# V weights loaded in two halves, the first V sum split around the next transposes and copied by ScalarE, one epsilon moved to VectorE

## Chip, cores, metric

One core of one Trainium2 chip. The metric is the device time of one launch in microseconds (us); lower is better. A profiled execution gives the span, from the first to the last instruction, which is 1.7 us less than the time.

## The reference, cut to what matters

```python
xn = layernorm(x)                       # x: 2048 x 512, bf16
qkv = xn @ wqkv                         # 512 x 1536; 32 heads of 16
p = softmax(where(window of 256 keys, q k^T / 4, -1e9))
out = x + (p v) @ wo + ((xn @ w_gate) * (xn @ w_up)) @ w_down      # F = 1792
```

The kernel works in chunks of 512 rows, each of four blocks of 128. The change is to the opening: the first chunk's normalisation, its transposes and its V projection.

## The kernel before

TensorE is called PE, ScalarE ACT, VectorE DVE, GpSimd POOL, SyncE SP. The parts that matter:

```python
# setup(): loads in order, all issued by SyncE
for lo, hi in ((0, 1), (1, 2), (2, 4)):
    nc.sync.dma_start(out=self.x[:, lo:hi, :], in_=xv[:, lo:hi, :])
for lo in (1024, 512, 0):                         # V, K, Q columns of Wqkv, 512 KB each
    nc.sync.dma_start(out=self.Wqkv[:, :, lo:lo + 512], in_=wq[:, :, lo:lo + 512])
# ... Wg, Wu, x 4:8, Wd, Wo ...
for lo, hi in ((8, 10), (10, 12), (12, NT)):
    nc.sync.dma_start(out=self.x[:, lo:hi, :], in_=xv[:, lo:hi, :])
# ...
self.keep_busy(40)                                # dummy 128x128 matmuls on zeros

def norm_transpose(self, t, by_dma):              # PE transposes, ScalarE copies to xnT
    # ...
    n = 2 if b == 0 else 4                        # block 0 in two pieces
    for lo in range(0, 4, n):
        ps = self.ps_m.tile([128, n, 128], BF16, tag="M", name="xTp")
        for k in range(n):
            nc.tensor.transpose(ps[:, k, :], xn[:, 128 * (lo + k):128 * (lo + k) + 128], self.ident[:])
        nc.scalar.activation(out=self.xnT[T][:, b, lo:lo + n, :], in_=ps[:], func=ACT.Copy)

def proj_v(self, t, ks=range(4), engine=None):    # V of block t: four matmuls over k, one copy
    # ...
    for k in ks:
        nc.tensor.matmul(ps[:], lhsT=self.xnT[T][:, b, k, :],
                         rhs=self.Wqkv[:, k, 1024:1536], start=(k == 0), stop=(k == 3))
    # ...

def first_chunk(self):
    # ... statistics, epsilon and power, xn of blocks 0 to 2 ...
    self.norm_transpose(0, False)
    self.keep_busy(8)
    for b in range(4):
        if b < 3:
            self.norm_transpose(b + 1, False)
        self.proj_v(b, engine="act" if b == 2 else "dve")
        if b == 0:
            self.norm_apply(3)
    self.proj_qk(0, 0, 1, engine="dve")           # K
    self.proj_qk(0, 0, 0, engine="act")           # Q
    self.swap_halves(0, self.nc.scalar)           # two transfers issued by ScalarE
    self.proj_qk(0, 1, 1, engine="dve")
```

After that the instructions of all engines follow a fixed list, the same in both kernels but for one x load.

The softmax here doesn't subtract the row's maximum and nothing guards it: scores larger than these inputs give would overflow.

## Time and profile before

| | kernel before |
|---|---|
| three timed runs, us | 264.74, 264.87, 264.91 |
| the profiled run: time, span | 265.39, 263.7 |
| V weights issued, landed in that run | 2.17, 7.13 |
| first V matmul, first K matmul in that run | 7.26, 11.35 |

How to read it: the prediction shows the lines. The first matmul of the K projection, which I call K below, is the end of the stretch that the change touches. From there PE works through the same list in both kernels.

### The profile page before, as it was taken

How to read it: one execution, taken by the hardware profiler on the slowest of the kernel's cores; microseconds unless marked ns; L12 is line 12 of the kernel's file. 1: busy time of each engine (PE TensorE's matmuls, PEld its weight loads, DVE VectorE, ACT ScalarE, POOL GpSimd, SP SyncE). 2: the span in 40 equal slices, each digit the busy share in tenths (PEclk: the TensorE clock that was granted, in tenths of full speed). 3: DMA queues.
4: the chain of work that ended last, by engine and by line, in shares of the span. 5: the costliest groups of instructions: out<-in, count | busy, mean ns of one | idle time of the engine just before them, and what ended most of it. 6: DMA issues, size and time to landing. Idle time of an engine off the chain costs nothing.

```text
span 263.7 us, 8896 instructions
## 1 busy us (share of the span) xinstructions
PE 259.4 (98%) x3890; PEld 120.9 (46%) x3890; DVE 175.1 (66%) x342; ACT 175.5 (67%) x141; POOL 116.9 (44%) x278
## 2 busy tenths in 40 slices
PE   8999999999999999999999999999999999999996
PEld 8444444444444544444544454444544445444453
DVE  6677888877845497567873669766685135977344
ACT  3376788888856866677776566767777546787600
POOL 6216342425457645334456644544453451463600
PEclk9999999999999999999999999999999999999999
DMA  6999921220002600002001310000100100000002
GB/s 180 378 357 340 281 29 22 24 47 4 0 25 57 84 2 0 4 0 47 5 0 42 81 45 2 0 2 19 32 4 0 42 21 22 5 0 2 4 2 80
DMA packets 19431, 15.12 MB, mean 57 GB/s; under 512 B 7360, under 2 KB 19392, under 8 KB 19392
## 3 DMA queue, kind: packets, MB, share of 16 engines
q1 hardware_dynamic: 18848, 14.26, 19.9%
q8 instruction: 30, 0.49, 0.8%
q10 hardware_dynamic: 544, 0.30, 0.4%
q14 instruction: 9, 0.07, 0.1%
HBM read 9.70 MB, written 2.10 MB: 45 GB/s over the span
## 4 chain that ended last, share of the span: by engine, by line
PE 96%; DMA 2%; SPq 0%; issue 0%; DVE 0%
PE gp L395 19%; PE up L406 19%; PE psd L428 17%; PE qkp L251 11%; PE S L312 10%; PE acc L366 6%; PE vp L239 5%; PE psd L434 5%; PE L L428 2%; DMA Wqkv<-in_A_wqkv_dram 2%; PE L L434 1%; PE L L366 0%; SPq L74 0%; PE xTp L209 0%; DVE x L444 0%
## 5 line engine op out<-in xcount | busy, mean ns | idle before, releaser
L319 ACT ACTIVATE P<-S 128x2048 bf16<-128x2048 f32 x75 | 140.7, 1876 | 50.6 <-PE S L312 46.8
L158 POOL TENSOR_SCALAR_AFFINE_SELECT P<-P 64x256 bf16<-64x256 bf16 x224 | 100.9, 450 | 126.3 <-ACT P L319 112.1
L395 PE MATMUL gp<-xnT,Wg 128*128 128x512 bf16 x224 | 60.1, 380 | 0.0
L406 PE MATMUL up<-xnT,Wu 128*128 128x512 bf16 x224 | 59.1, 380 | 0.0
L411 DVE TENSOR_TENSOR hT<-up,gsb 128x512 bf16<-128x512 f32 x56 | 38.3, 685 | 19.3 <-PE up L406 13.7
L428 PE MATMUL psd<-Wd,hT 128*128 128x512 bf16 (+1 forms) x210 | 48.0, 369 | 0.0
L343 DVE TENSOR_TENSOR P<-P,diag 128x512 bf16<-128x512 bf16 (+1 forms) x75 | 29.4, 392 | 6.1 <-ACT P L319 6.1
L428 PEld LDWEIGHTS <-hT 128*128 128x128 bf16 x238 | 21.3, 98 | 25.1 <-issue 2.9
L406 PEld LDWEIGHTS <-Wu 128*128 128x128 bf16 x224 | 20.5, 98 | 25.4 <-issue 2.5
L395 PEld LDWEIGHTS <-Wg 128*128 128x128 bf16 x224 | 20.3, 98 | 25.1 <-issue 1.9
L312 PE MATMUL S<-Q,K 16*64 16x320 bf16 (+4 forms) x720 | 31.0, 260 | 0.0
L312 PE MATMUL S<-Q,Ko 32*64 32x320 bf16 (+4 forms) x720 | 30.9, 260 | 0.0
L251 PE MATMUL qkp<-xnT,Wqkv 128*128 128x512 bf16 x128 | 29.9, 380 | 0.0
L230 ACT ACTIVATE gsb<-gp 128x512 bf16<-128x512 f32 x39 | 22.9, 596 | 8.2 <-PE gp L395 7.4
L312 PEld LDWEIGHTS <-K 16*64 16x64 bf16 x720 | 12.1, 103 | 30.7 <-issue 30.7
L372 DVE STREAM_TRANSPOSE at<-acc 128x512 f32<-128x512 f32 x30 | 19.1, 688 | 8.9 <-PE acc L366 8.9
L444 DVE TENSOR_TENSOR x<-psd,x 128x512 bf16<-128x512 f32 (+1 forms) x15 | 9.7, 655 | 15.7 <-PE psd L434 15.7
L251 PEld LDWEIGHTS <-Wqkv 128*128 128x128 bf16 x128 | 11.7, 98 | 14.5 <-issue 1.6
L366 PE MATMUL acc<-P,VS 64*32 64x320 bf16 (+4 forms) x672 | 17.7, 253 | 0.0
L366 PE MATMUL acc<-P,V 64*32 64x320 bf16 (+4 forms) x672 | 17.5, 253 | 0.0
L366 PEld LDWEIGHTS <-V 64*32 64x32 bf16 x720 | 15.1, 91 | 2.2 <-issue 1.6
L239 PE MATMUL vp<-Wqkv,xnT 128*128 128x512 bf16 x64 | 15.3, 380 | 0.5 <-DMA Wqkv<-in_A_wqkv_dram 0.5
(54 smaller groups left out, 200.2 us busy)
## 6 DMA issues: line engine op xcount, KB each, us to landing
out_dram<-x SPq DMA_DIRECT2D x15, 128.0 KB, 1.7
Wg<-in_B_w_gate_dram SPq DMA_DIRECT2D x2, 896.0 KB, 11.4
Wu<-in_B_w_up_dram SPq DMA_DIRECT2D x2, 896.0 KB, 13.7
Wd<-in_B_w_down_dram SPq DMA_DIRECT2D x1, 1792.0 KB, 17.2
Wqkv<-in_A_wqkv_dram SPq DMA_DIRECT2D x3, 512.0 KB, 5.9
x<-in_A_x_dram SPq DMA_DIRECT2D x2, 512.0 KB, 8.7
VS<-V SPq DMA_DIRECT2D x6, 144.0 KB, 2.6
x<-in_A_x_dram SPq DMA_DIRECT2D x3, 256.0 KB, 6.6
```

What stands on the lines that cost most here:

```text
L158: nc.gpsimd.affine_select(out=v, in_=v, pattern=pattern + [[1 if diag else -1, 64]], compare_op=ALU.is_ge if diag else ALU.is_gt, fill=0.0 ...
L230: nc.scalar.activation(out=out, in_=in_, func=ACT.Copy)
L239: nc.tensor.matmul(ps[:], lhsT=self.xnT[T][:, b, k, :], rhs=self.Wqkv[:, k, 1024:1536], start=(k == 0), stop=(k == 3))
L251: nc.tensor.matmul(ps[:], lhsT=self.Wqkv[:, k, lo:lo + 128], rhs=self.xnT[T][:, :, k, :], start=(k == 0), stop=(k == 3))
L312: nc.tensor.matmul(S[64 * par:64 * par + 64, e, col:col + n], lhsT=(self.Ko if par else self.K)[U, c][rows, keys], rhs=self.Q[T, c][rows, ...
L319: nc.scalar.activation(out=P[:, :, 0:col], in_=S[:, :, 0:col], func=ACT.Exp, scale=0.25)
L343: self.nc.vector.tensor_tensor(out=v, in0=v, op=ALU.min, in1=self.diag.unsqueeze(1).unsqueeze(1).to_broadcast([128, 4, n, 64]))
L366: nc.tensor.matmul(accs[par][32 * e:32 * e + 32, q:q + n], lhsT=v, rhs=P[rows, e, col:col + n], start=(i == 0), stop=(i == len(todo) - 1), ...
L395: nc.tensor.matmul(ps[:], lhsT=self.Wg[:, k, 128 * f:128 * f + 128], rhs=self.xnT[T][:, :, k, :], start=(k == 0), stop=(k == 3))
L406: nc.tensor.matmul(ps[:], lhsT=self.Wu[:, k, 128 * f:128 * f + 128], rhs=self.xnT[T][:, :, k, :], start=(k == 0), stop=(k == 3))
L411: nc.vector.tensor_tensor(out=self.hT[T, f][:], in0=ps[:], in1=self.gsb[:], op=ALU.mult)
L428: nc.tensor.matmul(ps, lhsT=self.hT[T, f][:, 128 * b:128 * b + 128], rhs=self.Wd[:, f, c0:c1], start=(f == 0), stop=False)
```

## The change

The intent: start the first V sum on two quarters of the weights before the rest has landed; put the next transposes between its halves; free VectorE of one copy, so that xn of block 3 comes sooner; shorten the chain to that xn by adding its epsilon on VectorE.

```diff
-        for lo in (1024, 512, 0):
-            nc.sync.dma_start(out=self.Wqkv[:, :, lo:lo + 512], in_=wq[:, :, lo:lo + 512])
+        for lo, ks in ((1024, slice(0, 2)), (1024, slice(2, 4)), (512, slice(0, 4)), (0, slice(0, 4))):
+            nc.sync.dma_start(out=self.Wqkv[:, ks, lo:lo + 512], in_=wq[:, ks, lo:lo + 512])
@@
-        for lo, hi in ((8, 10), (10, 12), (12, NT)):
+        for lo, hi in ((8, 12), (12, NT)):
@@ norm_scale: ve = var + epsilon
-        (nc.gpsimd if t else nc.vector).tensor_scalar(...)
+        (nc.vector if t in (0, 3) else nc.gpsimd).tensor_scalar(...)
@@ first_chunk
-        for b in range(4):
-            if b < 3:
-                self.norm_transpose(b + 1, False)
-            self.proj_v(b, engine="act" if b == 2 else "dve")
-            if b == 0:
-                self.norm_apply(3)
+        self.proj_v(0, (0, 1))
+        first = self.cur
+        self.norm_transpose(1, False)
+        self.cur = first
+        self.proj_v(0, (2, 3), engine="act")
+        self.norm_apply(3)
+        self.proj_v(1, (0, 1))
+        self.norm_transpose(2, False)
+        self.proj_v(1, (2, 3), engine="dve")
+        self.norm_transpose(3, False)
+        self.proj_v(2, engine="act")
+        self.proj_v(3, engine="dve")
```

More of the change, by code (lines that the diff above doesn't have):

```diff
@@ L178, in norm_scale @@
         ve = self.small.tile([128, n], F32, tag="ve", name="ve")
-        (nc.gpsimd if t else nc.vector).tensor_scalar(out=ve[:], in0=mv[:, :, 1], scalar1=1e-5, scalar2=None,
+        (nc.vector if t in (0, 3) else nc.gpsimd).tensor_scalar(out=ve[:], in0=mv[:, :, 1], scalar1=1e-5, scalar2=None,
                                                       op0=ALU.add)
```

## The prediction

> **What bounds the kernel now.** I read the busy table first, then the chain that ended last, then the waits of TensorE, then the first 15 us in order of time. From the page:
>
> ```profile
> span 263.7 us, 8896 instructions
> PE 259.4 (98%) x3890; PEld 120.9 (46%) x3890; DVE 175.1 (66%) x342; ACT 175.5 (67%) x141; POOL 116.9 (44%) x278
> PE   8999999999999999999999999999999999999996
> ```
>
> TensorE (PE) is busy 259.4 of 263.7 us, and only the first and last slice of forty (6.6 us each) show less than 9. No other engine passes 67%. The waits of PE, whole run:
>
> ```profile
> PE wps L127 <- DVE idle L94: 1.1, 1, 1.1
> PE vp L239 <- DMA Wqkv<-in_A_wqkv_dram: 0.5, 1, 0.5
> ```
>
> So PE waits twice: 1.1 us before its first dummy matmul, and 0.5 us before the first V matmul, for the V columns of Wqkv. From then to the last few us it is fed without a break. The chain in order of time, first 20 us, says the same:
>
> ```profile
> 2.17 4.96 DMA Wqkv<-in_A_wqkv_dram
> 7.12 0.14 issue
> 7.26 1.02 PE vp L239 x4
> 8.28 0.22 PE xTp L209 x4
> ```
>
> The V weights are issued at 2.17, land at 7.13, and PE starts on them 0.13 later. After that the chain is PE to the tail. Hence an earlier start of the projections is worth its full length at the end, but nothing else in this change touches the path. What the opening looks like, from the timeline (engine, line, operation; PE, ACT and DVE lines that matter):
>
> ```profile
> 5.74 0.76 PE L127 MATMUL wps<-idle 128*128 128x128 bf16 x8
> 5.88 0.41 DVE L190 TENSOR_SCALAR xn<-x,mv,rs 128x512 bf16<-128x512 bf16 x1
> 6.35 0.40 PE L209 MATMUL xTp<-ident,xn 128*128 128x128 bf16 x4
> 6.78 0.60 ACT L210 ACTIVATE xnT<-xTp 128x512 bf16<-128x512 bf16 x1 [0.36 <-PE xTp L209]
> 7.26 1.02 PE L239 MATMUL vp<-Wqkv,xnT 128*128 128x512 bf16 x4 [0.51 <-DMA Wqkv<-in_A_wqkv_dram]
> 8.93 0.40 DVE L190 TENSOR_SCALAR xn<-x,mv,rs 128x512 bf16<-128x512 bf16 x1
> 9.39 0.40 PE L209 MATMUL xTp<-ident,xn 128*128 128x128 bf16 x4
> 9.62 1.89 PE L239 MATMUL vp<-Wqkv,xnT 128*128 128x512 bf16 x8
> 11.35 2.75 PE L251 MATMUL qkp<-xnT,Wqkv 128*128 128x512 bf16 x12
> ```
>
> The start times give PE's true pace: the eight V matmuls from 9.62 to the first qkp at 11.35 take 1.73/8 = 0.216 us each, and four transposes (8.12 to 8.34, 9.39 to 9.62) 0.22 us together. The printed lengths add about 0.17 of pipeline at the end of each group. Between 7.26 and 11.35 lie 4.09 us; its work is 16 x 0.216 + 2 x 0.22 = 3.90 us. So two idle pieces exist before the K projection: 0.69 us between the transposes of block 1 (6.35 + 0.22 = 6.57) and 7.26, and some 0.19 us before the transposes of block 3 at 9.39. That last one waits for xn of block 3, which VectorE makes only at 8.93, behind the V copy of block 0. From 11.35 on the order of instructions is the same in both kernels on every engine (I compared the two built programs), apart from one x load.
>
> **What the Trainium skill says.** "TensorE: Matmul & The Clock Gate", section "Wait — 56ns, not 53.3ns?", gives 215.7 ns start to start for 512 columns and 55.6 for 128 when warm; the trace has 0.216 and 0.22/4 = 0.055, so it agrees. "DMA: Bandwidth & Descriptors", section "Why a DMA increments its semaphore by 16 and not by 1", says that only the full count means that all data landed. So today's first V matmul needs all 512 KB though it reads a quarter; two transfers give two completions. The trace agrees as far as it goes: one release at 7.13. The same page, "Anatomy of one DMA", puts most of the fixed cost in the receipt after the last byte, so half the bytes is not half the 4.96 us. "ScalarE: Activation LUTs", section "What ACT_TABLE_LOAD costs", has 186 ns + 0.833 ns per element, 0.61 us for 512 columns; the trace has 0.60 for both xnT and V copies, against 0.69 for a V copy on VectorE.
>
> **The change, part by part.** *V weights in two halves.* The three 512 KB pieces of Wqkv land 4.96 (V), 5.9 (K) and 6.9 us (Q) after their issues, which are 0.5 apart, so they land about 1.45 apart: 8.6 for K, 10.1 for Q. Half a piece at that pace is 0.73 us; at the 280 to 340 GB/s that the DMA shows between 5.0 and 6.5 us, 262 KB takes 0.8. So the first half should land at 7.13 - 0.8 = about 6.35 (estimate, 6.2 to 6.55), the second at 7.13 or slightly later. The additional issue on SyncE is some 0.45 us, while the queue already has a backlog: it costs nothing that is waited for. K is needed at 11.3 and lands at 8.6, Q at about 12.2 and lands at 10.1.
>
> *V sum of block 0 split.* New PE order: eight dummy matmuls (end of issue 6.35), V0 first half, transposes 1, V0 second half, V1 first half, transposes 2, V1 second half, transposes 3, V2, V3, then K. With S the start of V0's first half:
> - S = max(6.35, 6.35 + 0.13) = 6.48. Two matmuls: to S + 0.43 = 6.91.
> - Transposes 1 (xn of block 1 was ready at 6.29): 6.91 to 7.13, drained 0.18 later, ScalarE copies after 0.03 for 0.60: xnT1 at S + 1.46 = 7.94. Before it was 7.38: the split puts the transposes behind half of V0, and thereby makes this copy later by 0.56.
> - V0 second half at 7.26 to 7.69 (second half landed 7.13 + 0.13).
> - V1 first half waits for xnT1: S + 1.54 = 8.02 to 8.45. That is a new PE hole of 0.33.
> - Transposes 2: 8.45 to 8.67, drained 8.85, copy 8.88 to 9.48. ScalarE copies V0 meanwhile (about 7.94 to 8.54), which is out of the way in time.
> - V1 second half 8.67 to 9.10; transposes 3 from 9.10 to 9.32.
> - V2 waits for xnT2: 9.48 + 0.08 = 9.56 = S + 3.08, a hole of 0.24. V2 and V3: 8 x 0.216 = 1.73, to S + 4.81 = 11.29. xnT3 is ready by 10.1, before V3 needs it.
> So K starts at 11.29 instead of 11.35: a gain of 0.06 us. If the first half landed by 6.22, S is bounded by the dummies at 6.35, K is at 11.16, and the gain is 0.19: the most that this order gives. If it lands at 6.41 it is nothing, at 6.55 a loss of 0.14.
>
> *Epsilon of block 3 on VectorE.* PoolE's add takes 0.35 (7.20), VectorE's 0.15 for the same thing (3.84), and it saves one handover: rs about 0.3 us earlier, 7.9 instead of 8.20. With V0's copy gone from VectorE, xn of block 3 comes near 7.9 to 8.3 instead of 8.93 to 9.33. This takes away the wait of transposes 3 (now needed at 9.10), so 0.19 us of old hole; it is already in the sum above.
>
> *x of blocks 8 to 11 in one load.* It is issued at 25 us or later on a queue that then is far ahead of its readers (landing took 4.8 to 6.8 us). Zero.
>
> The sum: V0 starts 0.78 us earlier (7.26 - 6.48). Between its start and K lie now 4.81 us instead of 4.09: 0.22 more work (transposes 1 moved in), and holes of 0.13 + 0.33 + 0.24 = 0.70 instead of 0.19. So 0.78 - 0.22 - 0.51 = 0.05 to 0.06 us, with 0.19 as the ceiling. The landing estimate has its error on both sides, but the change was presumably kept for a gain, so I lean to the better side: 0.12 us. 264.87 - 0.12 = 264.75.
>
> **Rivals.**
> First, the full gain: the 0.51 us wait and the 0.19 hole vanish, 264.2. For it: PE alone sets the path after 7.26. Against: two handovers PE to ScalarE to PE of about 1.1 us each now stand with only two matmuls (0.43) and a half beside them.
> Second, a loss: the first half lands late (6.6 or later) because both halves share the engines' rings, or the transposes wait behind it; K then starts at 11.5 and the time is 265.0 to 265.1. For it: landings lag the bytes moved by nearly 1 us. Against: the transfer rate is level then.
> Third, the clock: the dummies' pace in the trace is 0.107 up to about 5.7 and 0.055 after 6.35, so full speed came near 6. V0's first half now sits close to that change. In a run where full speed comes later, two matmuls cost 0.2 us each more: 264.9 to 265.1. Against: the three runs agree within 0.17.
> Fourth, the load is hidden anyway and later waits absorb the shift: 264.87. Against: PE has no recorded wait after 7.26.
>
> **Range and chances.** The outcomes above lie between 264.2 and 265.1. Runs of one kernel spread by 0.17, another chip may add as much. I take 264.35 to 265.1 for 8 in 10. Two per cent are 5.3 us, ten times the whole hole in the opening; no part of the change can reach that: faster 0.005, same 0.985, slower 0.01.
>
> **What would show it.** In the profile after: the first vp near 6.5 with a short wait for Wqkv or none; the first transposes of block 1 after it at about 6.9; a PE wait on ScalarE's xnT before V1 (0.3) and V2 (0.2); no wait of transposes 3; xn of block 3 by 8.4; first qkp at 11.15 to 11.4, and everything after it moved by the same amount, scores at 14.0 as against 14.03. The prediction is wrong if the first qkp moves by over 0.3 us, if the first score does not move with it, or if a new wait of PE on a DMA appears after 12 us.

## The result, and the profile after

265.19 us, median of six runs (264.71 to 265.66); the kernel before, same rounds, 264.85 (264.73 to 265.43). The ratio is 1.001, interval 0.9995 to 1.0024. Within 2%, as predicted, but above the stated range (264.35 to 265.1), and where I had a gain of 0.12 us there is rather a loss of 0.3 (the interval just includes no change).

From the page of the changed kernel (busy time, then the busy tenths of PE):

```profile
span 263.6 us, 8878 instructions
PE 257.8 (98%) x3872; PEld 121.1 (46%) x3890; DVE 174.6 (66%) x342; ACT 176.0 (67%) x142; POOL 116.7 (44%) x277
PE   8999999999999999999999999999999999999995
```

18 of PE's 3890 matmul records are missing from this trace, which explains its lower busy sum and a few short waits for "issue" in its list; they are no idle time. The span is the same as in the profile before. The waits of PE on other engines:

```profile
PE wps L127 <- DVE idle L94: 1.1, 1, 1.1
PE vp L239 <- ACT xnT L210: 0.3, 1, 0.3
```

The wait for the V weights is gone and a wait for ScalarE's copy of xnT has come, as the prediction had it. The chain that ended last, in order of time, first 12 us:

```profile
1.07 4.45 PE wps L127 x40
5.52 0.43 PE xTp L209 x4
5.95 0.78 PE wps L127 x8
6.72 0.21 PE vp L239
...
7.42 0.61 ACT xnT L210
...
9.59 1.90 PE vp L239 x8
```

Before, the chain began with the transfer of the weights. Now it begins with the dummy matmuls: the eight of them end at 6.56, when the first V matmul starts, though its weights had landed at 5.51 and both pieces of its operand were copied by 6.43 (the first, which is all it needs, at about 6.1). And the V sum of block 1 stands behind ScalarE's copy. In this trace K is at 11.32, which is S + 4.76 with S = 6.56; I had put S + 4.81.

So the opening went much as I had worked it out. The signs that the prediction named for the profile came as well: xn of block 3 at 7.99, the first score at 14.01, no new wait for a DMA. K came 0.03 earlier than in the profile before, and yet the timed runs are slower. All these signs were set against the one profile before, so that is where this pointed.

### The profile page after: what moved, and what is told of

It reads as the page before. It is cut to its first block, busy times and chain, and to the rows that moved or that the text cites. A ratio compares the mean times of both kernels' runs of the same rounds, so it can differ in the third digit from the quotient of the medians.

```text
span 263.6 us, 8878 instructions
## 1 busy us (share of the span) xinstructions
PE 257.8 (98%) x3872; PEld 121.1 (46%) x3890; DVE 174.6 (66%) x342; ACT 176.0 (67%) x142; POOL 116.7 (44%) x277
## 4 chain that ended last, share of the span: by engine, by line
PE 98%; issue 1%; ACT 0%; DVE 0%
PE gp L401 19%; PE up L412 19%; PE psd L434 17%; PE qkp L251 11%; PE S L318 10%; PE acc L372 6%; PE vp L239 5%; PE psd L440 5%; PE L L434 2%; PE wps L127 2%; PE L L440 1%; PE xTp L209 0%; PE L L372 0%; ACT xnT L210 0%; DVE x L450 0%
## 5 line engine op out<-in xcount | busy, mean ns | idle before, releaser
L434 PE MATMUL psd<-Wd,hT 128*128 128x512 bf16 (+1 forms) x198 | 46.1, 368 | 1.4 <-issue 1.1
```

What stands on the lines that cost most here:

```text
L434: nc.tensor.matmul(ps, lhsT=self.hT[T, f][:, 128 * b:128 * b + 128], rhs=self.Wd[:, f, c0:c1], start=(f == 0), stop=False)
```

## The experiments

Theories. A: the profile before is a slow sample, the V weights usually land half a us sooner, so the old order usually reaches K well before 11.35, and the new order's serial copies cost about what they seemed to save. B: in the new order the dummies are on the path, so each run follows the moment at which PE reaches full pace. The rivals are with each run. All runs gave a correct result. The first 12 ran in three batches of four on three chips, the last four on a fourth chip with one look each.

V landing is when the trace shows the load complete (for cut loads, each piece in the order of its place in V). S is the start of V0, in the old order behind the transposes of block 1. K is the start of the first K matmul, all in us.

| run | median | ratio to before (interval) | V landed | S | K | span of the trace |
|---|---|---|---|---|---|---|
| before, given profile | 264.87 | | 7.13 | 7.26 | 11.35 | 263.7 |
| after, given profile | 265.19 | 1.001 (0.9995 to 1.0024) | 5.5 and 6.45 | 6.56 | 11.32 | 263.6 |
| before_again | 264.79 | 1.0001 (0.9989 to 1.0013) | 6.5 | 6.64 | 10.74 | 263.0 |
| after_again | 265.26 | 1.0016 (1.0002 to 1.0029) | 5.7 and 7.79 | 6.27 | 11.51 | 263.8 |
| halves_only | 265.04 | 1.0009 (0.9997 to 1.0021) | 5.7 and 7.74 | 6.64 | 11.45 | 263.9 |
| after_one_load | 266.12 | 1.0044 (1.0031 to 1.0057) | 6.60 | 6.73 | 11.49 | 263.9 |
| after_two_dummies | 266.37 | 1.0053 (1.004 to 1.0065) | 5.4 and 7.25 | 5.92 | 10.96 | 264.1 |
| after_16_dummies | 267.9 | 1.0111 (1.0093 to 1.0128) | 5.3 and 7.46 | 6.83 | 11.59 | 265.9 |
| before_16_dummies | 266.89 | 1.008 (1.0065 to 1.0095) | 6.6 | 6.79 | 10.88 | 265.2 |
| after_old_order | 265.2 | 1.0014 (1.0001 to 1.0026) | 5.4 and 7.36 | 6.59 | 10.98 | 263.3 |
| eps_only | 264.94 | 1.0002 (0.9989 to 1.0015) | 6.6 | 6.73 | 10.82 | 263.1 |
| x_merged_only | 264.96 | 1.0002 (0.999 to 1.0014) | 6.5 | 6.69 | 10.79 | 263.8 |
| after_moved_dummies | 265.23 | 1.0011 (0.9999 to 1.0023) | 5.7 and 7.41 | 6.16 | 11.12 | 263.4 |
| moved_two_queues | 266.08 | 1.0044 (1.0025 to 1.0063) | 6.82 and 4.0 | 6.96 | 11.72 | 264.6 |
| before_third (one look) | 264.95 | | 6.7 | 6.81 | 10.90 | 263.2 |
| halves_again (one look) | 264.92 | | 5.6 and 6.2 | 6.64 | 10.73 | 263.2 |
| k_halves (one look) | 265.05 | | 6.4 | 6.78 | 10.88 | 263.3 |
| v_quarters (one look) | 265.13 | | 4.8, 5.7, 7.0 and 7.32 | 6.64 | 10.81 | 263.4 |

A check on the whole table: span minus K is 252.3 to 252.6 in thirteen of the eighteen traces. The other five are those with an added wait after K, named below. So K stands for the end, and it is read more sharply than the time.

### before_again: the kernel before, unchanged

> The kernel before, unchanged: how far do its own runs differ? Theory A (the profile of before was a slow sample: its profiled run took 265.39, the timed ones 264.87): the V weights land at 6.5 to 6.7 here, the first V matmul starts before 6.9, the first K matmul at 10.7 to 10.9 instead of 11.35, span about 263.2. Rival (it was a typical run): landing at 7.1, K at 11.3, span 263.7. Ratio 1.000 either way.

Timeline of PE in this second profile of the kernel before (start, length, engine, line, operation):

```profile
5.44 0.61 PE L127 MATMUL wps<-idle 128*128 128x128 bf16 x8
6.40 0.40 PE L209 MATMUL xTp<-ident,xn 128*128 128x128 bf16 x4 [0.35 <-DVE xn L190]
6.64 1.02 PE L239 MATMUL vp<-Wqkv,xnT 128*128 128x512 bf16 x4
10.74 1.46 PE L251 MATMUL qkp<-xnT,Wqkv 128*128 128x512 bf16 x6
```

V landed at 2.17 + 4.3 = 6.5, no wait for it is listed, K is at 10.74, 0.61 before that of the first profile. V0 follows the transposes of block 1, which follow xn of block 1: the bracket says that PE sat idle 0.35 us for VectorE. The eleven runs of before in this batch lie between 264.77 and 265.03; the given profile, at 265.39, is outside them. Of all 45 other runs of before three are as slow (265.43, 265.57, 266.13). Theory A holds. The trace before_third agrees (6.7, 10.90).

The load is hidden only just. In the first profile V0 starts 0.14 after V's landing (7.12 to 7.26); it starts equally long after it in before_again (6.51 to 6.64), before_third (6.68 to 6.81) and eps_only (6.59 to 6.73). In the last two PE stood idle some 0.1 us for it, too short for the list of waits.

### after_again: the changed kernel, unchanged

> The changed kernel, unchanged. Theory A with B (the dummy matmuls are now on the path, so a run follows the moment at which TensorE gets its full clock): ratio 1.001 to 1.002 and a spread of nearly 1 us over its runs, wider than that of the kernel before; K at 11.0 to 11.5 according to the pace of the eight dummies. Rival (only noise): ratio within 0.9995 to 1.0005, both spreads alike.

```profile
5.74 0.69 PE L127 MATMUL wps<-idle 128*128 128x128 bf16 x8
6.27 0.59 PE L239 MATMUL vp<-Wqkv,xnT 128*128 128x512 bf16 x2
7.83 1.02 PE L239 MATMUL vp<-Wqkv,xnT 128*128 128x512 bf16 x4 [0.75 <-DMA Wqkv<-in_A_wqkv_dram]
```

The loss repeats, with a spread of 264.8 to 266.07. Two things differ from the first trace of this kernel. The dummies took 0.69 instead of 0.99, so S came 0.29 earlier; and the second half of V landed only at 7.79, so PE waited 0.75 for it. K is at 11.51. The fastest runs of both batches (264.71, 264.8) equal the floor of the kernel before. By the constant of the table they should have K near 10.75, which needs S near 6.0: an estimate, no such run was traced.

### halves_only: the kernel before with two loads

```diff
-        for lo in (1024, 512, 0): ...
+        for lo, ks in ((1024, slice(0, 2)), (1024, slice(2, 4)), (512, slice(0, 4)), (0, slice(0, 4))): ...
```

> The kernel before with the V load in two halves, order of before. Theory A: V0 follows the transposes of block 1 at once, at 6.6 to 6.8, and K comes at 10.6 to 10.8 whatever the second half does; 0.0 to 0.3 us faster than before, ratio 0.999 to 1.000. Rival (two loads cost: a later landing of the second half, or the later issues): slower, ratio 1.001.

Not what theory A expected: the ratio 1.0009 is unclear but rather slower, and in the trace V0 starts at 6.64 and then stops half way for the rest of the weights:

```profile
6.64 0.59 PE L239 MATMUL vp<-Wqkv,xnT 128*128 128x512 bf16 x2
7.78 0.59 PE L239 MATMUL vp<-Wqkv,xnT 128*128 128x512 bf16 x2 [0.55 <-DMA Wqkv<-in_A_wqkv_dram]
```

The profiled run is the slowest of its five (265.59; the others 264.86 to 265.15), so it shows the mechanism and not its usual size.

### after_one_load: the changed kernel with V in one load

```diff
-        for lo, ks in ((1024, slice(0, 2)), (1024, slice(2, 4)), (512, slice(0, 4)), (0, slice(0, 4))): ...
+        for lo in (1024, 512, 0): ...
```

> The changed kernel with the V load in one piece again. If the serial order of copies is what costs (theory A): V0's first half waits for the landing at 6.6 to 7.1, then the chain S + 4.8 puts K at 11.5 to 12.0: slower than the changed kernel by 0.2 to 0.5 us, than before by 0.5 to 1.0, ratio 1.002 to 1.004. Rival (the order costs nothing, the halves cost): ratio 1.000.

This gives the price of the order alone, at a landing that is as usual for one load (6.60):

```profile
6.73 0.59 PE L239 MATMUL vp<-Wqkv,xnT 128*128 128x512 bf16 x2 [0.33 <-DMA Wqkv<-in_A_wqkv_dram]
7.38 0.59 PE L239 MATMUL vp<-Wqkv,xnT 128*128 128x512 bf16 x2
8.24 0.60 PE L239 MATMUL vp<-Wqkv,xnT 128*128 128x512 bf16 x2 [0.26 <-ACT xnT L210]
```

K is at 11.49, 0.75 after that of before_again, with V0 started 0.09 later. The chain from S to K is 4.76 against 10.74 - 6.64 = 4.10 in the old order; 0.22 of the difference is the transposes of block 1, which the old order has done before V0, the rest is waiting for ScalarE's copies. In time it is 1.0044, some 1.2 us; the profiled run (265.6) is near the fast end of its five (to 266.25), and what makes the slower ones 0.6 longer was not traced. The rival is out: the order costs. By time the halves win back some 0.7 us in that order (1.0044 against 1.0016 in the same batch); by K the traces show 0.17 in after and nothing in after_again (11.32 and 11.51 against 11.49), so most of the 0.7 lies in what was not traced.

### The dummies: after_two_dummies, after_16_dummies, before_16_dummies

```diff
-        self.keep_busy(8)
+        self.keep_busy(2)        # after_two_dummies;  16 in the two others
```

> The changed kernel with 2 dummies instead of 8 ahead of V0's first half. Theory B (the dummies are on the path of the changed kernel): V0 starts at about 6.2, when its first operand has been copied, instead of 6.27 to 6.56, so K comes up to 0.4 us earlier where the second half of V lands in time; median 264.8 to 265.0, ratio to before 1.000 to 1.0007. Rival (they are not): as the changed kernel, 265.2, ratio 1.0015.

> The changed kernel with 16 dummies. Theory B: 8 more cost 8 x 0.055 to 8 x 0.107 = 0.44 to 0.86 us at the start of V0 and most of it at the end (less where the second half of V was late anyway): ratio to before 1.002 to 1.004, K at 11.5 to 12.1. Rival: 1.0015, as with 8.

> The kernel before with 16 dummies. There they stand beside the wait for xn of block 1 (ready at 6.35 in the second trace of before, the dummies done at about 5.87): 8 more fit in wholly when the clock is full early, and cost 0.1 to 0.4 us when it is full late. Ratio 1.000 to 1.001, clearly less than the same 8 cost in the changed kernel. Rival (dummies cost the same in both): 1.002 to 1.003.

By K, theory B holds. With two dummies S is at 5.92, the earliest of all, and K at 10.96 although the second half of V came at 7.25; with sixteen S is at 6.83 and K at 11.59, again S + 4.76. In the kernel before, sixteen moved K from 10.74 to 10.88 only. By time, every expectation was wrong, by up to 2 us. The waits of PE in before_16_dummies show why:

```profile
PE qkp L251 <- issue: 0.8, 1, 0.8
PE up L406 <- issue: 0.8, 1, 0.8
```

These are stalls late in the kernel, in which PE waits for nothing that the profile names. In both traces with sixteen they lie at about 94 and 129 us, just before the 1376th and the 1888th matmul of PE; with two dummies there is one, at 189 us, before the 2784th. All three numbers leave 96 when divided by 128, so the stalls come at one place of a period of 128 matmuls. In before_again PE is busy without a break in the same stretch. So these three times say nothing of the opening, and only K can be used.

### after_moved_dummies: the same number of PE instructions again

```diff
-        self.keep_busy(8)
+        self.keep_busy(2)
         self.proj_v(0, (0, 1))
         first = self.cur
         self.norm_transpose(1, False)
+        self.keep_busy(6)
         self.cur = first
```

> The changed kernel with 2 dummies ahead of V0's first half and the other 6 moved behind the transposes of block 1, where TensorE waits anyway: the number of TensorE instructions is again that of the changed kernel. Theory C (with 2 or 16 dummies the added stalls of 0.5 to 1.5 us at 93, 128 and 189 us came from the changed number of instructions): none of these here, span minus K start 252.2 to 252.5. Theory B: V0 starts at 5.9 to 6.2, K at 10.9 to 11.2 with the second half of V at 7.2 to 7.8, ratio 1.000 to 1.001. Rival (the stalls come from the place of the dummies): stalls here too, ratio 1.004 or more.

Theory C holds: no stall, span minus K is 252.3. The stalls came with the number of PE's instructions, not with the place of the dummies. S is at 6.16 and K at 11.12, held by the second half of V:

```profile
6.16 0.60 PE L239 MATMUL vp<-Wqkv,xnT 128*128 128x512 bf16 x2 [0.25 <-ACT xnT L210]
7.45 1.02 PE L239 MATMUL vp<-Wqkv,xnT 128*128 128x512 bf16 x4
```

That is the earliest K of the traced runs that have the new order and 8 dummies, but its time (ratio 1.0011) is not better than that of the changed kernel beyond the noise.

### after_old_order: everything but the split of the sum

```diff
-        self.proj_v(0, (0, 1)) ... # the twelve lines of the change
+        for b in range(4):
+            if b < 3:
+                self.norm_transpose(b + 1, False)
+            self.proj_v(b, engine="act" if b in (0, 2) else "dve")
+            if b == 0:
+                self.norm_apply(3)
```

> Everything of the change but the split of the V0 sum: two loads, epsilon by VectorE, V0 copied by ScalarE, transposes of block 1 ahead of V0 as before. If the serial order of copies is what costs (theory A): K at 10.6 to 10.9 when the second half lands in time, about 0.3 us faster than the changed kernel, ratio to before 0.9995 to 1.0005; if the second half lands at 7.7 again, K at 11.4 and the order made no difference. Rival (ScalarE's V0 copy costs, since it stands ahead of the xnT copy of block 2): K at 11.0 or later, ratio 1.001 or more.

Between the two expectations. K at 10.98 is 0.34 and 0.53 before the two traces of the changed kernel, and V0's second part started at 7.40, behind the second half of V, which landed at 7.36. But the timed ratio, 1.0014, is no better than that of the changed kernel, and two loads in the old order were at 1.0009. Here ScalarE copies V0 (8.10) ahead of xnT of block 2 (8.59), which holds the V sum of block 2 to 9.24, so the rival has a part, at most the 0.10 us that PE stands idle there. With two loads the order is worth less than with one, since both orders then wait for the late half.

### eps_only and x_merged_only: the two small parts alone

```diff
+ eps_only:       (nc.vector if t in (0, 3) else nc.gpsimd).tensor_scalar(...)
+ x_merged_only:  for lo, hi in ((8, 12), (12, NT)):
```

> The kernel before with the epsilon of block 3 added by VectorE. My prediction: xn of block 3 sooner, and so K up to 0.19 us sooner. Seen in the second trace of before, the wait of transposes 3 is only 0.1 us and VectorE stands in front of xn of block 2, so the 0.15 us add delays transposes 2 by about as much: K within 0.1 of 10.74, ratio 0.9995 to 1.0005.

> The kernel before with blocks 8 to 11 of x in one load. Prediction and theory A: nothing, K at 10.7 to 10.8, ratio 0.9995 to 1.0005. Rival (a later load moves and a reader waits): over 1.001. Its V load is one more sample of the landing in one piece (6.5 to 6.7 expected, 7.1 in one trace of five).

Both at 1.0002, no difference that these runs can see. In eps_only VectorE's line is the point:

```profile
7.18 0.15 DVE L179 TENSOR_SCALAR ve<-mv 128x1 f32<-128x1 f32 x1
7.27 0.41 DVE L190 TENSOR_SCALAR xn<-x,mv,rs 128x512 bf16<-128x512 bf16 x1
```

The add stands in front of xn of block 2, which starts at 7.27 instead of 7.11 (before_again), and the transposes of block 2 at 7.74 instead of 7.58. Without the other parts xn of block 3 stays behind V0's copy, at 8.40.

The trace of x_merged_only holds a surprise that has nothing to do with x. Its profiled run (265.54) is 0.4 to 0.65 us above the other four, with K at 10.79. ScalarE took long to issue its two swap transfers (2.38 us in all against 1.34 in before_again, the second alone 1.68), so its first exponential came 1.1 us late and PE waited:

```profile
17.15 0.28 PE L312 MATMUL S<-Q,K 16*64 16x192 bf16 x4 [0.56 <-ACT P L319]
```

This is one way in which a single run can end late; moved_two_queues shows it too (2.35 us for the two issues, a wait of 0.5).

### moved_two_queues: the second half of V issued by ScalarE

```diff
+        nc.scalar.dma_start(out=self.Wqkv[:, 2:4, 1024:1536], in_=wq[:, 2:4, 1024:1536])   # after the warm exponential
```

(on top of after_moved_dummies, with SyncE's second half removed)

> The same with the second half of V issued by ScalarE at about 2.3 us, beside SyncE's first half. Theory D (in two loads the second half lands later, 7.2 to 7.8 against 6.5 to 7.1 for the one load, because it is issued behind the first): it lands by 6.9, V0's second half starts by 7.0, K at 10.6 to 10.9, ratio 0.999 to 1.0003, the best version so far. Rival (the later landing has to do with two loads as such): 7.2 or later again and K at 10.9 or later.

```profile
0.96 0.43 ACTq L93 DMA_DIRECT2D Wqkv<-in_A_wqkv_dram  x1
6.96 0.59 PE L240 MATMUL vp<-Wqkv,xnT 128*128 128x512 bf16 x2 [0.70 <-DMA Wqkv<-in_A_wqkv_dram]
```

Theory D's landing came true and its gain did not. ScalarE issued its half at 0.96, before the exponential (2.08) and not at 2.3, and it landed first, at 4.0. But V0 begins with SyncE's half, which now landed at 6.82 instead of 5.3 to 5.7. The x loads came later as well (the first transposes started at 5.69 instead of 5.2 to 5.3). K is at 11.72, the ratio 1.0044. The last byte of V came 0.6 earlier than in after_moved_dummies (7.41), but the half that is needed first came last. A run with the first half issued by ScalarE was not made.

### before_third, halves_again, k_halves, v_quarters: is a cut load always later?

Each is the kernel before with other loads (in one, the same):

```diff
+ k_halves:    (1024, slice(0, 4)), (512, slice(0, 2)), (512, slice(2, 4)), (0, slice(0, 4))
+ v_quarters:  *((1024, slice(k, k + 1)) for k in range(4)), (512, slice(0, 4)), (0, slice(0, 4))
```

> The kernel before, a third trace: V lands whole at 6.5 to 6.6 (5 of 6 traces so far), K at 8.3 to 8.6, first K matmul at 10.7 to 10.8, span 263.1.

> V in two loads in the order of before, a second trace: if the later landing is the rule, second half at 7.2 to 7.8, first half at 5.4 to 5.7; if the first trace was a slow sample, 6.6.

> V in one load, K in two. If cutting a load makes its own end later: V at 6.5 to 6.6 as before, K's second half at 9.1 or later instead of 8.3 to 8.6. If what counts is that later loads are issued later: V unchanged and K unchanged within 0.3. K is read at 10.7 only, so the time stays at 264.8 to 265.0.

> V in four loads, order of before. If each cut costs: the last quarter at 8 us or later, first K matmul at 11.6 or later, about 266. If two loads cost for another reason: last quarter at 7.2 to 7.8 as with two.

Mostly, not always. In halves_again the second half landed at 6.2 and K came at 10.73. In k_halves the second half of K landed at 8.3 (issued at 3.24, 5.0 later), not later than a whole K. In v_quarters, on the same chip, the last quarter landed at 7.32, as the second expectation had it; it is needed last, so V0's last matmul came only some 0.07 late (7.36), too short for the list of waits. So the late half is frequent (7.2 to 7.8 in six of the eight traces whose second half of V follows the first on SyncE) but not a rule. Nor is it that half alone: in seven of these eight the K weights landed at 8.9 to 10.2 (10.18 in after, whose half came at 6.45), against 8.2 to 8.95 in the eight traces with V in one piece. Nothing waited for them. What decides it was not found.

No experiment pointed to a version that beats both kernels: in the usual run of the kernel before, V0 starts 0.24 us (up to 0.36 where V lands last) after the transposes that xn of block 1 releases, and what is left until K is the 3.90 us of work and 0.2 us of holes.

## Why the prediction was wrong, point by point

**What bounds the kernel: right, but read from an unusual run.** PE sets the path and the V load was the one wait, in that profile; I had no second one. In the seven other traces with V in one piece (before_again, before_third, after_one_load, before_16_dummies, eps_only, x_merged_only, k_halves) V landed at 6.4 to 6.7 instead of 7.13. In the six of them that have the old order K is at 10.74 to 10.90, and what is left of the 0.51 us wait is some 0.1 in two of them.

**The failing step is the sum, in its first term.** I had "V0 starts 0.78 us earlier (7.26 - 6.48)". In the usual run V0 starts at 6.64 to 6.81 before the change, and after it at 6.56 and 6.27: earlier by 0.1 to 0.5 us only, against a chain that is longer by 0.67 (4.76 against 4.09; I had 0.72). And I wrote "264.87 - 0.12 = 264.75": a gain measured against K = 11.35, taken off a median whose runs have K near 10.8. With the same chain and the usual K it reads 11.29 - 10.74 = 0.55 us slower, 265.4. Measured were 265.19 and 265.26, so the truth lies nearer to that. The sign was decided by which run had been profiled, and the two numbers that showed it, 265.39 for the profiled run and 264.91 for the slowest timed one, were given.

**The chain of copies: right.** S + 4.81 was predicted, 4.76 measured in three traces (after, after_one_load, after_16_dummies), with the waits of V1 and V2 for xnT where they were put (0.42 and 0.20 us in after; I had 0.33 and 0.24). My first rival, the full gain, fell to exactly that.

**S: right in size by accident.** I had S = 6.48, from a first half landing at 6.35. It landed at 5.5 to 5.7. What held S were the dummies, 6.56 and 6.27; my third rival named their pace, but put its cost on the two V matmuls behind them. The eight took (0.99 - 0.17)/8 = 0.10 us each in after and (0.61 - 0.17)/8 = 0.055 in before_again. In the kernel before, the wait for xn of block 1 covers most of that difference: in k_halves, with 0.98 for the eight, the transposes of block 1 began at 6.56, 0.16 later than in before_again, and K was at 10.88. In the changed kernel all of it goes to the start of V0. In the batch of after_again this fits the spreads: 1.27 us for the changed kernel, 0.26 for the kernel before. It is not all there is to spreads: in the two later batches single runs of before reached 266.13 and 265.57.

**The second half of V: wrong.** I had "7.13 or slightly later", as for the whole load. It was 6.45 in one trace of the changed kernel and 7.79 in the other. Where late, it added up to 0.75 us of waiting, so that not all of the early start of V0 could be used even in principle.

**Epsilon and x: the first half right.** Transposes 3 no longer wait, and xn of block 3 started at 7.99 in the changed kernel. That the add delays xn of block 2 by 0.16 I did not see. The merged x load is worth nothing that can be measured, as said.

**What stays open**: why the second half of V, and K behind it, is late in most traces; how much of the 0.3 us is the order and how much the late half in an average run (after_one_load shows the order's price where V comes whole; halves_only at 1.0009 is not resolved); and the 0.6 us between runs of after_one_load.

## What to carry to other kernels

Before you take a wait from a profile, set the time of the profiled run beside the timed ones: if it lies outside them, the wait may be its peculiarity, and a gain worked out against it must not be taken off the median. When you fill the gap ahead of a wait with work, ask what the gap was covering: here it hid the slow pace of the warm-up matmuls and the time of ScalarE's copies, and both came onto the path once it was closed. And when an experiment changes the number of instructions, judge it by the time of an event close to the change, and check that the distance from there to the end has stayed the same.

## What the Trainium skill lacked or had wrong

- "Runtime: NRT & Kernel Launch", section "Instruction fetch mechanics", says that crossing a 16 KiB instruction block is mostly hidden. Adding 8 dummies to PE gave two stalls of about 0.8 us in before_16_dummies and of 1.1 and 0.5 us in after_16_dummies, with no engine or transfer to wait for. Their period of 128 matmuls, which with the weight loads are 256 instructions, fits such a block. But in none of the five stalls did the trace's instruction queue move anything: its last transfer ended 0.4 to 0.8 us before, the next began 1.1 us after. So that they are instruction fetches is not shown.
- "DMA: Bandwidth & Descriptors", section "Latency and other measured facts", gives an HBM latency of 0.2 us on average and 2 us under load, but no spread for the landing of one and the same load: 512 KB issued at 2.17 landed at 6.4 to 7.13, the second of two halves, issued at 2.68, at 6.2 to 7.79. Nor has it a spread for the issue on the engine that issues: two swap transfers occupied ScalarE's issue for 1.34 us in one run and 2.38 in another, and the exponential behind them came that much later.
- No page says that warm-up matmuls can come to stand on the path: in the new order V0 started at 5.92 and 6.16 with 2 of them ahead of it, at 6.27 and 6.56 with 8, and at 6.83 with 16.
